# Two more chunks with all of their first layer in seven products, second weight sums in buffers of their own, some gates on GpSimd, longer filler matmuls

## The chip, the cores and the metric

The kernel runs on one core of one Trainium2 chip. A core has a matrix engine (TensorE, PE in the profile; its weight loads are PEld), three engines for elementwise work (VectorE, DVE; ScalarE, ACT; GpSimd, POOL), a queue engine (SyncE, SP) and 16 DMA engines that move data between the device memory and the core's SBUF. Matmul results land in PSUM banks, which DVE and ACT read and POOL does not.

The metric is the device time of one execution in microseconds, the median of several runs; lower is better.

## The reference

Linear attention with a cosine reweighting, and then two dense layers with a gate. All inputs are float32.

```python
# q, k, v: [8 batches, 8 heads, 576 positions, 64]
theta = pi / 2 * pos / 576
phi(x) = concat([max(x, 0) * cos(theta), max(x, 0) * sin(theta)])    # 64 -> 128
kv  = sum over s of phi(k)[s]^T v[s]                                 # 128 x 64 for each head
z   = sum over s of phi(k)[s]
att = (phi(q) @ kv) / (phi(q) @ z + 1e-6)
x   = att, heads side by side                                        # 4608 tokens x 512
h   = x @ w_in                                                       # 512 -> 2048
out = (h * cos(h)) @ w_out                                           # 2048 -> 512
```

## The kernel before

**Chunks.** Of each batch's 576 tokens 512 form a chunk of their own; the 64 that are left over of all eight batches form a ninth chunk (number 8, buffer xR). For each batch the kernel loads q, k and v (tiles qm, km, vm), makes phi with one instruction for each tile and half (`prep`, on ACT or DVE, output KQ), casts v to 16 bits (`cast_v`), forms kv and z in one product (`kv`, L371), transposes phi(q) (`q_pe` on PE for batches 0 and 1, `q_dma` as a DMA transpose later), multiplies (`num`, L433) and normalises (L449 to L453, on DVE), and transposes the result into xT (`x_pe` or `x_dma`). In batches 1, 3, 5 and 7 there is a fifth tile of q, which holds the left-over tokens of two batches.

**First layer, plain.** A column block of w_in (128 of 2048 columns) takes four matmuls of 512 columns (L562) into a PSUM bank; chunks 0 and 1 use matmuls of 256 (L530). Its gate is a Sin on ACT with a phase of a quarter turn (L503, output ch) and a multiplication (L505, `mul`) that writes gT.

**First layer in seven products.** From chunk 3 on, the dictionary FAST1 says how many of the four column groups of a chunk are formed by a Strassen-like scheme (`layer1_fast`): seven products of four 256-column matmuls (L666) take the place of four plain blocks of four 512-column ones. The scheme needs sums of parts of x (`layer1_sums`, tiles XS) and of w_in (`w_in_sums`, tiles WS): the first set (f = 0) serves groups 0 and 1, the second (f = 1) groups 2 and 3. Partial results are copied by ACT into SBUF (Y, U, Z; L674) and completed by additions on DVE (L678). Four gates follow in two narrow and one double-width multiplication: one of Y (512 columns, both inputs in SBUF, L505), one of U and Z together (1024 columns, both inputs in SBUF, L695), and one read from a PSUM bank (L505). In the kernel before, FAST1 gives two groups to chunks 3, 4, 5, 6 and 8 and four to chunk 7, and the second set of sums lies in the four buffers of the transposed q tiles (qT), since all attention is done by then.

**Second layer.** Seven products again for all chunks but the first (`layer2`, L860), with sums of the gated values (L836, L897) on DVE, or by accumulating DMAs for chunks 6 and 7 (L818). Results go to three output buffers (ost) and by DMA to the output; the stores of chunks 4, 5 and 6 add in memory (L744 and L748).

**Order of the work.** Each step of the program is recorded with `pl.add`, and two tables written out in the kernel say the rest: STARTS, a number for each step by which all steps are sorted, and ENGS, the engine of each step. So the order on each engine is fixed before the program runs, and an engine executes its list strictly in that order. Steps marked `port=True` on DVE and POOL additionally wait for each other: whenever the next marked step is on the other engine, a semaphore makes it wait for the marked step before it. DMAs are issued from the lists of SP and POOL, in order too: an issue that waits holds up what stands behind it.

**Start.** While q of batch 0 is loaded, PE runs filler matmuls on a constant tile (`warm`, L944), a second filler follows the transposes of q, and short ones stand between the first steps of `num`. The loads of w_in (four quarters, POOL queue) are held back until k of batch 0 has landed. The loads of batch 1 are held back by tiny copies on POOL (`hold_raw`, L974) that read the third quarter of w_in, the one the tables call number 2.

Of the kernel before, what the change touches and what calls it, by code (L numbers as in the profile page):

```python
# [181 lines left out]
def kernel(  # L182
# [90 lines left out]
    PAIRS0, PAIRS1 = (None, PAIRS[1]), (None, PAIRS[3])  # L273
    FILL = (4, 3, 2, 0)

    Q_PE, X_PE = (), range(1, 3)
    VCAST = ("DVE", "ACT")
    LAZY = 8.0
    LATE_BY, LATE_W = (0.0, 1.0, 3.0, 1.0), 0.6
# [111 lines left out]
    def qdst(b, t):  # L391
        return (qT[t], ("qT", t)) if t < NT else (qT4, ("qT4", 0))
# [730 lines left out]
```

## Time and profile before

| what | value |
|---|---|
| median of 3 runs | 283.02 us (282.95 to 283.87) |
| profiled execution, its own time | 285.63 us |
| span of the profiled execution, first to last instruction | 283.9 us |
| mean granted TensorE clock | 0.984 |
| PE matmuls | 2635, busy 272.2 us (96%) |
| DVE busy | 241.3 us (85%) |
| ACT busy | 205.3 us (72%) |
| POOL busy | 57.7 us (20%) |

Times of the profile are microseconds from the span's start. A line of a group names the source line, engine, operation, output and input tile, shape and count, then the busy time and the mean duration of one in ns, and then the idle time just before such instructions with what ended it. Matmuls overlap, so the mean duration of one is longer than the distance from one to the next; how many are issued in a stretch is read from the time line. A line of the time line gives start, length, engine and count; in square brackets stands the engine's idle time before it and who ended it.

### The profile page before, as it was taken

How to read it: one execution, taken by the hardware profiler on the slowest of the kernel's cores; microseconds unless marked ns; L12 is line 12 of the kernel's file. 1: busy time of each engine (PE TensorE's matmuls, PEld its weight loads, DVE VectorE, ACT ScalarE, POOL GpSimd, SP SyncE). 2: the span in 40 equal slices, each digit the busy share in tenths (PEclk: the TensorE clock that was granted, in tenths of full speed). 3: DMA queues.
4: the chain of work that ended last, by engine and by line, in shares of the span. 5: the costliest groups of instructions: out<-in, count | busy, mean ns of one | idle time of the engine just before them, and what ended most of it. 6: DMA issues, size and time to landing. Idle time of an engine off the chain costs nothing.

```text
span 283.9 us, 6672 instructions
## 1 busy us (share of the span) xinstructions
PE 272.2 (96%) x2635; PEld 210.9 (74%) x2635; DVE 241.3 (85%) x447; ACT 205.3 (72%) x357; POOL 57.7 (20%) x87
## 2 busy tenths in 40 slices
PE   7699999999999999999999999999999999999993
PEld 2557857669976677877867777787768888876882
DVE  1666798999999999997989999999998979987742
ACT  2646699589989979998988959995736687676030
POOL 1322020021500310140150102415101343230410
PEclk9599999999999999999999999999999999999998
DMA  6999989969999999999998999989323949693515
GB/s 190 316 189 241 256 270 217 354 192 242 238 341 240 262 226 191 209 339 258 291 229 199 216 324 200 220 189 163 102 57 95 180 120 110 172 134 67 113 74 148
DMA packets 80222, 58.01 MB, mean 204 GB/s; under 512 B 43200, under 2 KB 77248, under 8 KB 80192
## 3 DMA queue, kind: packets, MB, share of 16 engines
q1 hardware_dynamic: 68960, 39.99, 59.0%
q0 software_dynamic: 10496, 17.04, 28.4%
q10 hardware_dynamic: 736, 0.57, 0.7%
q8 instruction: 20, 0.33, 0.5%
q14 instruction: 10, 0.08, 0.1%
HBM read 36.75 MB, written 11.80 MB: 171 GB/s over the span
## 4 chain that ended last, share of the span: by engine, by line
PE 77%; DMA 10%; DVE 5%; ACT 3%; issue 1%; POOL 1%; SPq 1%; ACTq 0%; DVEq 0%
PE M L860 28%; PE M L562 10%; PE M L530 9%; PE M L666 9%; PE M L785 5%; PE TR L666 4%; DMA qT<-KQ 3%; DMA vm<-in_v_dram 3%; PE ATT L433 3%; PE TR L562 2%; PE ATT L371 2%; DMA qm<-in_q_dram 2%; DMA out_dram<-ost 2%; PE M L400 2%; PE ATT L944 2%
## 5 line engine op out<-in xcount | busy, mean ns | idle before, releaser
L860 PEld LDWEIGHTS <-gT 128*128 128x128 f16 x560 | 54.4, 98 | 10.1 <-issue 0.8
L503 ACT ACTIVATE ch<-M 128x512 f32<-128x512 f32 x85 | 49.8, 596 | 11.4 <-PE M L530 5.0
L860 PE MATMUL M<-w_out_sb,gT 128*128 128x256 f16 x448 | 57.1, 273 | 0.5 <-ACT ost L871 0.5
L505 DVE TENSOR_TENSOR gT<-M,ch 128x512 f16<-128x512 f32 x78 | 52.1, 685 | 5.1 <-ACT ch L503 5.0
L871 ACT ACTIVATE ost<-M 128x512 f32<-128x512 f32 x41 | 24.3, 597 | 21.8 <-PE M L860 17.7
L344 ACT ACTIVATE KQ<-km,CS 128x512 f16<-128x512 f32 x56 | 38.5, 719 | 1.3 <-DMA km<-in_k_dram 1.3
L562 PE MATMUL M<-xT,w_in_sb 128*128 128x512 f16 x160 | 39.1, 379 | 0.0
L344 ACT ACTIVATE KQ<-qm,CS 128x512 f16<-128x512 f32 x49 | 33.8, 718 | 5.2 <-DMA qm<-in_q_dram 5.2
L562 PEld LDWEIGHTS <-w_in_sb 128*128 128x128 f16 x224 | 21.1, 98 | 17.7
L860 PE MATMUL M<-T,S 128*128 128x256 f16 x256 | 32.2, 273 | 0.0
L530 PE MATMUL M<-xT,w_in_sb 128*128 128x256 f16 x256 | 30.2, 273 | 0.8 <-DVE gT L505 0.8
L360 POOL CAST V<-vm 128x1024 f16<-128x1024 f32 (+1 forms) x18 | 15.9, 912 | 68.7 <-DMA vm<-in_v_dram 24.0
L860 PEld LDWEIGHTS <-S 128*128 128x128 f16 x256 | 24.8, 98 | 4.1
L530 PEld LDWEIGHTS <-w_in_sb 128*128 128x128 f16 x256 | 24.4, 98 | 4.4 <-issue 0.7
L666 PEld LDWEIGHTS <-w_in_sb 128*128 128x128 f16 x216 | 20.7, 98 | 3.4
L453 DVE TENSOR_TENSOR x<-ATT,rec 128x512 f16<-128x512 f32 x32 | 22.1, 692 | 1.3 <-DVE rec L451 0.2
L731 POOL DMA_DIRECT2D out_dram<-ost x20 | 10.8, 545 | 48.8 <-ACT ost L871 35.9
L678 DVE TENSOR_TENSOR Z<-M,Z 128x512 f32<-128x512 f32 x26 | 17.6, 686 | 2.4 <-PE M L666 1.2
L433 PEld LDWEIGHTS <-qT 128*128 128x128 f16 (+1 forms) x320 | 14.3, 101 | 5.1 <-issue 1.9
L674 ACT ACTIVATE Z<-M 128x512 f32<-128x512 f32 x22 | 12.9, 597 | 6.6 <-PE M L666 6.4
L748 POOL DMA_DIRECT2D out_dram<-ost x12 | 6.7, 566 | 52.9 <-ACT ost L871 52.9
L503 ACT ACTIVATE ch<-TR 128x512 f32<-128x512 f32 x17 | 10.2, 599 | 9.4 <-PE TR L666 5.0
(144 smaller groups left out, 473.8 us busy)
## 6 DMA issues: line engine op xcount, KB each, us to landing
out_dram<-ost POOLq DMA_DIRECT2D x38, 256.0 KB, 4.0
qm<-in_q_dram SPq DMA_DIRECT2D x8, 640.0 KB, 6.7
km<-in_k_dram SPq DMA_DIRECT2D x8, 640.0 KB, 7.0
qm<-in_q_dram SPq DMA_DIRECT2D x8, 512.0 KB, 5.7
km<-in_k_dram SPq DMA_DIRECT2D x8, 512.0 KB, 5.3
vm<-in_v_dram SPq DMA_DIRECT2D x6, 640.0 KB, 7.4
vm<-in_v_dram SPq DMA_DIRECT2D x6, 512.0 KB, 7.0
w_in_sb<-in_moe_w_in_dram POOLq DMA_DIRECT2D x4, 512.0 KB, 9.1
```

Source lines behind the costliest of these rows:

```text
L344: fn = {"ACT": lambda: nc.scalar.activation(out=out_, in_=in_, func=AF.Relu, scale=sc), "DVE": lambda: nc.vector.tensor_scalar(out=out_, i ...
L360: "POOL": lambda: nc.gpsimd.tensor_copy(out=out_, in_=in_)}
L433: nc.tensor.matmul(bank[hb][ps, hh * D1:(hh + 1) * D1], lhsT=x[:, h, :], rhs=z[:, h, :], start=True, stop=True)
L453: nc.vector.tensor_tensor(out=split(x16[n][:, hs, :], k), in0=A[:, :, :, 0:D], in1=split(rec[n][:, hs], k).unsqueeze(3).broadcast_to((P, k ...
L503: act(0.5, due, lambda: nc.scalar.activation(out=ch[c], in_=bank, func=AF.Sin, bias=math.pi / 2.0, scale=1.0), [key], [("ch", c)])
L505: mul(due, 0.61, lambda q: q.tensor_tensor(out=dst, in0=bank if len(dst.shape) == 2 else bank.rearrange("p (j s) -> p j s", j=dst.shape[1] ...
L530: nc.tensor.matmul(M1[m][:, jj * 2 * P:(jj + 1) * 2 * P], lhsT=w_in_sb[:, cc, j * P:(j + 1) * P], rhs=X[:, cc, ts], start=(cc == 0), stop= ...
L562: nc.tensor.matmul(M, lhsT=w_in_sb[:, cc, j * P:(j + 1) * P], rhs=X[:, cc, :], start=(cc == 0), stop=(cc == NCT - 1))
L666: nc.tensor.matmul(bank[0][:, j * TH:(j + 1) * TH], lhsT=a(cc, j), rhs=b[:, cc, :], start=(first and j == 0 and cc == 0), stop=(last and j ...
L678: dve(0.61, due + 0.3, lambda: nc.vector.tensor_tensor(out=dst, in0=bank[0], in1=dst, op=ALU.add), [bank[1], key], [key])
L860: nc.tensor.matmul(bank[0][:, tt * MH:(tt + 1) * MH], lhsT=a[:, j, tt * P:(tt + 1) * P], rhs=b[:, j, :], start=(first and (apart or tt == ...
L871: act(0.5, due, lambda: nc.scalar.activation(out=dst, in_=view(bank), func=AF.Copy), [bank[1]], dk)
```

## The change

- **FAST1**: chunk 6 and chunk 8 form all four groups in seven products, as chunk 7 did. 16 plain blocks become four groups of seven products.
- **w_in's second sums** get buffers of their own (WSB2 to WSB4, and a part of w_in that is no longer read), and are formed ahead of chunk 6 where they were formed ahead of chunk 7. To make room, the fifth tile of transposed q has no buffer of its own any more (qT4 is gone): it uses that of tile 0. Its transpose is therefore recorded after the products of the other tiles.
- **Gates on GpSimd**: the multiplications of Y and of U with Z may be on DVE or POOL, and the tables say which. 10 of 18 gates of Y and 5 of 18 of U with Z are on POOL: in chunk 8 four of Y and two of U with Z, the others in chunks 3 to 7.
- **Filler**: the first from 14 to 28 matmuls, the second from 16 to 17.
- **The tables** are new as a whole, 1363 steps where there were 1335, so the order changes on every engine. PE has 2698 matmuls for 2635. At the start the order is now: filler, transposes of q tiles 3 and 0, second filler, transpose of tile 1, first half of `kv`, second half, transpose of tile 2, `num`; before, all four transposes stood ahead of the second filler and `kv` behind it. DVE's and ACT's copies of transposed q stand behind k's preparations and v's casts, where two of them stood between. w_in's quarters are loaded in the order 0, 1, 3, 2 (before: 2, 0, 1, 3), with the first half of w_out behind them and `hold_raw`, which waits for quarter 2, behind that. After batch 1's `kv` PE now has one transpose, four halves of `num`, one transpose and then a step of the second layer; before, two transposes, the same halves of `num` and that step.

The diff, with the two tables left out:

```diff
@@ -241,7 +244,6 @@
     KQ = sb("KQ", [P, 2, (NT + 1) * H * 2 * D])
     kp, qp = [KQ[:, n].rearrange("p (t h g d) -> p t h g d", t=NT + 1, h=H, g=2) for n in range(2)]
     qT = [sb(f"qT{t}", [P, H, P]) for t in range(NT)]
-    qT4 = sb("qT4", [P, H, P])
     kvz = [sb(f"kvz{n}", [P, H, D1]) for n in range(2)]
     NX = 4
     den = [sb(f"den{n}", [P, H], F32) for n in range(NX)]
@@ -273,7 +275,7 @@
     PAIRS0, PAIRS1 = (None, PAIRS[1]), (None, PAIRS[3])
     FILL = (4, 3, 2, 0)
 
-    Q_PE, X_PE = (), range(1, 3)
+    X_PE = range(1, 3)
     VCAST = ("DVE", "ACT")
     LAZY = 8.0
     LATE_BY, LATE_W = (0.0, 1.0, 3.0, 1.0), 0.6
@@ -389,7 +391,7 @@
                 out=Z, in_=ATT[:, :, 0:HB * D1], func=AF.Copy), keys, zk)
 
     def qdst(b, t):
-        return (qT[t], ("qT", t)) if t < NT else (qT4, ("qT4", 0))
+        return qT[t % NT], ("qT", t % NT)
 
     def q_pe(b, t, bank, key, eng, due):
         dst, dkey = qdst(b, t)
@@ -488,14 +490,11 @@
     m1n, chn, m2n = [0], [0], [0]
 
     def mul(due, cost, fn, rd, wr, pool):
-
         if pool is None:
             dve(cost, due, lambda: fn(nc.vector), rd, wr)
-        elif pool:
-            pl.add("POOL", 0.15 + 1.9 * cost, 0.3 + 1.9 * cost, due, lambda: fn(nc.gpsimd), rd, wr,
-                   port=True)
         else:
-            dve(cost, due, lambda: fn(nc.vector), rd, wr, port=True)
+            either(due, {"DVE": cost, **({"POOL": 0.15 + 1.9 * cost} if pool else {})},
+                   {"DVE": lambda: fn(nc.vector), "POOL": lambda: fn(nc.gpsimd)}, rd, wr)
 
     def gate(bank, key, dst, dkeys, due, pool=None, rd=()):
         c = chn[0] % NCH
@@ -566,23 +565,25 @@
              rd=["KQ"] if c == B else [])
 
 
-    FAST1 = {3:2,4:2,5:2,6:2,7:4,8:2}
+    FAST1 = {3:2,4:2,5:2,6:4,7:4,8:4}
     SUMS_AT = min(FAST1) - 1
-    Y_POOL, UZ_POOL = (), ()
+    Y_POOL, UZ_POOL = range(B + 1), range(B + 1)
     CH2, JF = NCT // 2, JH * P // 2
 
 
     WSA = {1: w_in_sb[:, 0:CH2, 2 * JF:3 * JF]}
     for n in (2, 3, 4):
         WSA[n] = sb(f"WS{n}", [P, CH2, JF])
-    LATE = any(nf > 2 for nf in FAST1.values())
+    LATE = min(c for c, nf in FAST1.items() if nf > 2)
+    assert all(FAST1[c] == NJT // 4 for c in range(LATE, NC))
 
     def flat(t, dt=F16):
         v = t.rearrange("p a b c -> p (a b c)") if len(t.shape) == 4 else t.rearrange(
             "p a b c d -> p (a b c d)")
         return v if dt == F32 else v.bitcast(F16)
-    WSB = {n: qT[n - 1].rearrange("p h s -> p (h s)").rearrange("p (c f) -> p c f", c=CH2)
-           for n in range(1, 5)}
+    WSB = {1: w_in_sb[:, 0:CH2, 3 * JF:4 * JF]}
+    for n in (2, 3, 4):
+        WSB[n] = sb(f"WSB{n}", [P, CH2, JF])
 
     Z3 = [sb("Z3", [P, 3 * SM], F32)]
     XSS = [[sb(f"XS{i}", [P, CH2, TH]) for i in range(4)]]
@@ -600,9 +601,9 @@
 
         def tt(n, a, b, op, rd, wr):
             dve(0.61, due, lambda: nc.vector.tensor_tensor(out=ws[n], in0=a, in1=b, op=op),
-                [("w_in", f), ("w_in", 2 + f)] + rd, wr + [("WS", n, f)] + ([("qT", n - 1)] if f else []), lazy=20.0, port=True)
+                [("w_in", f), ("w_in", 2 + f)] + rd, wr + [("WS", n, f)], lazy=20.0, port=True)
         tt(3, a11, a21, ALU.subtract, [], [])
-        tt(1, a21, a22, ALU.add, [], [] if f else [("w_in", 2)])
+        tt(1, a21, a22, ALU.add, [], [("w_in", 2 + f)])
         tt(2, ws[1], a11, ALU.subtract, [("WS", 1, f)], [])
         tt(4, a12, ws[2], ALU.subtract, [("WS", 2, f)], [])
 
@@ -988,7 +989,7 @@
         for i, nm in enumerate("kv"):
             dve(0.53, i - 9, lambda nm=nm: nc.vector.memset(raw[nm][:, :, NT, :], 0.0), [],
                 hk(nm, ts=[NT]))
-        warm(14, 6.5)
+        warm(28, 9.05)
         for nm in ORDER0:
             load(0, nm, 0, HALVES if nm == ORDER0[2] else (slice(0, H),))
         weights()
@@ -996,7 +997,7 @@
             prep(0, "q", t, 0, "DVE", t)
             prep(0, "q", t, 1, "DVE" if t == 1 else "ACT", t)
             q_pe(0, t, *BANKS[t], "ACT" if t % 2 else "DVE", t)
-        warm(16, 3.45, rd=[("TR", 0)])
+        warm(17, 3.67, rd=[("TR", 0)])
         for t in range(NT + 1):
             prep(0, "k", t, 0, "DVE", 4)
             prep(0, "k", t, 1, "DVE" if t == 2 else "ACT", 4)
@@ -1027,13 +1028,16 @@
             due = T + 2 + t + 6 * (t > 1)
             for g in range(2):
                 prep(1, "q", t, g, "DVE" if g == 0 else "ACT", due)
-            q_pe(1, t, *BANKS[t % 2], "ACT" if t % 2 else "DVE", due)
+            if t < NT:
+                q_pe(1, t, *BANKS[t % 2], "ACT" if t % 2 else "DVE", due)
         for hb in range(2):
             for t in range(NT + 1):
                 cast_v(1, t, "ACT" if t % 2 else "DVE", T + 4 + hb, HALVES[hb])
         kv(1, T + 6)
         for t in range(NT + 1):
             due = T + 8 + t if t < NT else start[1] + 12
+            if t == NT:
+                q_pe(1, t, *BANKS[t % 2], "ACT" if t % 2 else "DVE", due - 2)
             n = num(1, t, due, PAIRS1[t % len(PAIRS1)])
             x_pe(1, t, n, *BANKS[t % 2], "ACT", due)
 
@@ -1051,12 +1055,12 @@
             due = T + 8 + 1.2 * t
             for g in range(2):
                 prep(b, "q", t, g, "", due)
-            if b in Q_PE:
-                q_pe(b, t, TR, ("TR", 0), "ACT" if t % 2 else "DVE", due + 1)
-            else:
+            if t < NT:
                 q_dma(b, t, due + 1)
         for t in list(range(NT)) + ([NT] if b % 2 else []):
             due = start[b] - 9 + 1.2 * t if t < NT else start[b]
+            if t == NT:
+                q_dma(b, t, due - 3)
             n = num(b, t, due)
             if b in X_PE:
                 x_pe(b, t, n, TR, ("TR", 0), "ACT", due)
@@ -1074,7 +1078,7 @@
             attention(c)
         if c == SUMS_AT + 1:
             w_in_sums(0, start[c] - 12)
-        if c == B - 1 and LATE:
+        if c == LATE:
             w_in_sums(1, start[c] - 6)
         layer2(c - 1)
         layer1(c)
```

More of the change, by code (lines that the diff above doesn't have):

```diff
@@ L117 @@
     "DDPSSSSSSSSGGGGGGGGDAPDDDPADAPDDAPAPDADADDDADADADADDADADPPADPPDPPAPPDPPAPPDPPAPPDPAPADPADP"
-    "ADPADPADPADPADPADPADPADPADPADPADPADPADPADGSSGSSGGGGGSSSSDADADADADADAPDDAPADAPDDAPADAPDDADA"
-    "DDADADPPAPPDPAPPDPAPPDPAPPDPAPPDPAPAPAPAPAPDPDGGPDPDGGPADPADPADPADPADPADPADPADPADPADPADPAD"
-    "PADPADPADPADDDDDSSSSSSAADDADADDAGGGPPADDSAASADSDASPPDPAPPDPAPPDPAPPDPADDDPPAPPDDPPAPPAPPDP"
-    "PDGGPPAGGPADPADPADPADPADPADPADPADPADPADPADPADPADPADPADPADSSSSSSAAAAAAADADGGGPPAAASADSAASAD"
-    "SAASPPDSPPDSPPDSPPDSPPDSDDDDDDDPPAPPDDPPAPPAPPDPPDGGPPAGGDDDDPAPDADPAPAPDPDADPADPADPADPADP"
@@ L129 @@
-    "DDDDDDSPPAPPAGGPPAGGPPAPPAPPAGGPPAGGGGDDDDPAPDADPAPAPDPDADPADPAPDADPAPAPDPDADPADPAPDADPAPA"
-    "PDPDADPADPAPDADPAPAPDPDADPADDDDDSPPAPPDGGPPAPPAPPDPPDGGPPAGGDDDDPAPDADPAPAPDPDADPADPADPADP"
-    "ADPADPAPDADPAPAPDPDADPADPADPADPADPADDDDDDDPPAPPDDDPPAPPAPPDPPDSASAAPPDSADSA"
+    "ADPADPADPADPADPADPADPADPADPADPADPADPADPADGSSGSSGGGGGSSSSDADADADADADAPDDAPADAPDDAPADADADADD"
+    "ADADPPAPPDPAPPDPAPPDPAPPDPAPDPPDPAPAPAPAPAPDPDGGPDPDGGPADPADPADPADPADPADPADPADPADPADPADPAD"
+    "PADPADPADPADDDDDSSSSSSADADAADDAAGGGPPADASDDSAASAASPPDPAPPDPAPPDPAPPDPADDDPPAPPDDPPAPPAPPDP"
@@ new lines @@
+    "PDGGPPAGGPADPADPADPADPADPADPADPADPADPADPADPADPADPADPADPADSSSSSSDDAAAAAAAAGGGPPADASAASDASAA"
+    "SADPPDSPPDSPPDSPPDSSPPDSDDDDDDDPPAPPDDPPAPPAPPDPPDGGPPAGGDDDDPAPDAGPAPAPDPDADPADPADPADPADP"
+    "ADPAPDAGPAPAPDPDADPADPADPADPADPADSSSSSSAAAAAADAAAGGGPPAAASAASAASADSPPDSPPDSPPDSPPDSDDDPPAP"
+    "PDDPPAPPAPPDPPDGGPPAGGDDDDPAPDAGPAPAPDPDADPADPADPADPADPADPAPDADPAPAPDPDADPADPADPADPADPADSS"
+    "SSSSDDAAAAAAADGGGPPAADSAASDDSAASAAPPDSPPDSPPDSPPDSSPPDSDDDPPAPPADPPAGGPPAPPAPPAGGPPAGGGGDD"
+    "DDPAPDAGPAPAPDPDADPADPADPADPADPADPAPDADPAPAPDPDAGPADPADPADPADPADSSSSSSAAAAAAADAAGGGPPAAASA"
@@ new lines @@
+    "DSADSAASPPDSPPDSPPDSPPDSDDDDDDDPPAPPADPPAGGPPAPPAPPAGGPPAGGGGDDDDPAPDADPAPAPDPDADPADPAPDAG"
+    "PAPAPDPDAGPADPAPDADPAPAPDPDADPADPAPDADPAPAPDPDADPADSSSSSSDAAAAAAAAAGGGPPADASDASAASDDSAAPPD"
+    "SPPDSPPDSPPDSSPPDSDDSPPAPPAGGPPAGGPPAPPAPPAGGPPAGGGGDDDDPAPDAGPAPAPDPDAGPADPAPDADPAPAPDPDA"
+    "DPADPAPDADPAPAPDPDADPADPAPDADPAPAPDPDADPADDDDDSPPAPPDGGPPAPPAPPDPPDGGPPAGGDDDDPAPDAGPAPAPD"
+    "PDAGPADPAPDAGPAPAPDPDAGPADPAPDAGPAPAPDPDADPADPAPDAGPAPAPDPDADPADDDDDDDPPAPPDDDPPAPPAPPDPPD"
+    "SASAAPPDSADSA"
```

6 lines of the change are left out of this document (removed), and 194 rows, old and new, of the table STARTS.

## Prediction

> **What bounds the kernel now.** I read the page first: TensorE (PE) is busy for 96% of the span, and its idle times are few.
>
> ```profile
> span 283.9 us, 6672 instructions
> PE 272.2 (96%) x2635; PEld 210.9 (74%) x2635; DVE 241.3 (85%) x447; ACT 205.3 (72%) x357; POOL 57.7 (20%) x87
> PEclk9599999999999999999999999999999999999998
> ```
>
> Then the table of windows, for the start and three long stretches (busy us, then instructions; the last three columns are granted clock, DMA share, GB/s):
>
> ```profile
> 5.10:8.50 3.40, 1.26 (x6) 0.39 (x4) 0.14 (x1) 0.17 (x1) 0.00 (x0) 1.00 1.02 359
> 8.50:15.30 6.80, 5.92 (x38) 4.28 (x39) 5.60 (x13) 5.46 (x10) 3.27 (x5) 0.50 0.93 272
> 46.00:130.00 84.00, 83.58 (x896) 62.57 (x893) 79.58 (x154) 72.84 (x128) 14.57 (x20) 1.00 1.05 258
> 130.00:188.00 58.00, 57.48 (x563) 45.42 (x563) 53.73 (x98) 50.70 (x90) 10.59 (x16) 1.00 1.03 237
> 188.00:278.00 90.00, 90.00 (x825) 74.52 (x824) 76.63 (x123) 52.28 (x91) 24.21 (x30) 1.00 0.60 118
> ```
>
> From 46 us on PE misses under 1 us in all, so there a microsecond taken from PE's list is a microsecond gained, as long as DVE (85 to 95% busy) and POOL keep up. Before 46 us it is another matter: PE waits for data, and from 8.5 to 15.3 us it has half its clock. The time line of PE shows what that costs:
>
> ```profile
> 9.38 1.01 PE L400 MATMUL TR<-IDENT,KQ 128*128 128x128 f16 x8 [3.02 <-DVE KQ L345]
> 10.19 2.76 PE L400 MATMUL M<-IDENT,KQ 128*128 128x128 f16 x24
> 12.75 4.90 PE L944 MATMUL ATT<-S 128*128 128x512 f16 x16
> 17.48 1.38 PE L371 MATMUL M<-V,KQ 128*128 128x65 f16 x40
> 23.67 1.04 PE L530 MATMUL M<-xT,w_in_sb 128*128 128x256 f16 x8
> ```
>
> The 16 filler matmuls (L944) hold PE until 17.3 us, though v has landed (13.2 us its first heads, 14.7 us the rest, by the landing records). Last, the groups by shape, for the gates and for POOL:
>
> ```profile
> L505 DVE TENSOR_TENSOR gT<-M,ch 128x512 f16<-128x512 f32 x78 | 52.1, 685 | 5.1 <-ACT ch L503 5.0
> L695 DVE TENSOR_TENSOR gT<-Z,ch 128x1024 f16<-128x1024 f32 x9 | 11.0, 1220 | 0.2 <-ACT ch L689 0.2
> L360 POOL CAST V<-vm 128x1024 f16<-128x1024 f32 x12 | 12.5, 1057 | 55.5 <-DMA km<-in_k_dram 20.8 <-DVE den L449 18.5 <-DMA vm<-in_v_dram 10.8
> L360 POOL CAST V<-vm 128x512 f16<-128x512 f32 x6 | 3.7, 620 | 13.2 <-DMA vm<-in_v_dram 13.2
> L744 POOL DMA_DIRECT2D out_dram<-ost x12 | 12.2, 1383 | 6.7 <-ACT ost L871 4.1 <-DMA out_dram<-ost 2.6
> ```
>
> The sum is made against the profiled execution: span 283.9, its own time 285.63, so 1.7 lie around the span. It is 2.6 above the median of the three runs, 283.02; I subtract the same difference from the median. About 0.3% (0.85 us) is what a measurement of this kernel can tell from no change.
>
> **Part 1, seven products.** Two column groups each of batch 6 and of the last chunk change. Plain: 16 matmuls of 512 columns, issued 8 in 1.73 us, 3.45. Seven products: 28 of 256 columns, 8 in 0.874, 3.06. Four groups: **-1.6 us** of PE. Their weight loads (98 ns) fit under a 109 ns matmul. ACT gets +1.7 a group (three copies and a wide Sin against four Sins), beside PE: 17 of 27 us busy at 188 to 215, 14 at 242 to 269. DVE gets 4.65 for 2.74 a group (three additions at 0.69, gates 0.68, 1.22 and 0.69), +7.6; ten gates of 512 and five of 1024 leave it for POOL, -12.9. So DVE gets 5 us shorter, though not in each stretch: at 188 to 215 it is busy 26.3 of 27. The second sums (4 at 0.6) only move earlier.
>
> **Part 2, the start.** The first filler goes from 14 to 28 matmuls. In this trace nine ran at 0.427 until 5.1 us, later ones take 0.216: 28 end at 5.1 + 19 x 0.216 = 9.2 us, just ahead of the transposes that wait for q's preparation until 9.38. In the trace the clock fell after a stretch (5.1 to 8.5) in which PE was busy for 1.26 us of 3.40; now that stretch is full, and I expect the clock to stay at 1.0. Then, by the new order: two transposed tiles at 0.46 (to 10.3), 17 fillers at 0.216 (to 14.0), a third tile (14.4). DVE no longer copies a q tile between k's preparations: five at 0.40 from 11.6, three casts at 0.2, one preparation, 14.7; ACT ends its share at 14.8. kv starts at 14.9 instead of 17.48, and its second half at 15.5. From kv to the first layer the trace has 6.2 us (17.48 to 23.67); the new order moves one more tile transpose into waits there, so the first layer starts at about 21.4 for 23.67.
>
> What is late next? Batch 1's loads. They wait, behind a POOL instruction, for quarter 2 of w_in, which is now the fourth load, not the first. The first two quarters landed at 18.1 and 20.7, 2.6 apart while nothing else ran; so the fourth lands at 25.9, where loads were issued from 18.8 before. The first half of w_out needs 5.2 more at that rate, k, q and v 10.5 (batch 0's three took 11.9 with 2 of latency): last v at 41.6, against 42.3 before. The order is worse, the end no later. PE by its own list reaches batch 1's second kv half at 21.4 + 0.46 + 16 x 0.87 + 3 x 1.73 + 2 x 0.46 + 0.62 = 42.5, plus 1.1 of idle as before: 43.6. Before it was 46.18, with 0.46 more work ahead: 2.1 gained. Then a loss: before, a second-layer step of 1.73 stood early enough to cover kvz's copy and the normalisations; now part of it is bare, 0.2 to 1.5, I take 0.8. Net **-1.3 us**; from both sides 0 (v late by 2 us, or the clock halved after all) and -2.4.
>
> **Part 3, gates on POOL.** The trace has no two-input operation on POOL. From below: DVE's own rows, 0.68 and 1.22. From above: two casts that read as much, 2 x 0.62 = 1.24 and 2 x 1.06 = 2.11. I take the upper ends, since a cast of equal reads on the same engine is the nearest row. Each gate stands in one line with DVE's instructions marked for the shared port: the next marked one on DVE waits for POOL, and all DVE behind it. Nine of the fifteen lie in chunks 3 to 7, one or two to a chunk: such a turn is some 0.6 (1.24 less 0.68) to 0.9 us longer than DVE's own, which the 5 us that DVE is spared hide. The tight place is the last chunk: by the program's order PE has, between its first POOL gate and the first second-layer product that needs the last one, 18 first-layer products at 0.44 and eight second-layer steps at 0.87, 14.9 us, of which about 14.5 lie after that gate's start; POOL's queue holds 4 gates of 512, 2 of 1024, a pair of accumulating DMAs (2.47 by the pair at 249.4) and two single ones (1.38): 4.96 + 4.22 + 2.47 + 2.76 = 14.4. It just fits: **+0.2**, from 0 to +1.5. The Trainium skill, GPSIMD Engine Reference, section 3.1, measures a two-input addition at 1.96 times DVE's time: 1.34 and 2.39 here as an estimate, 15.4 us for that queue, and the sum would be 0.8 higher.
>
> **Part 4, batch 1, 3, 5 and 7's fifth q tile** now reuses the first tile's buffer: it waits for that tile's products, and SP's queue (loads and transposes behind it) with it. In the trace this transpose took SP 1.3 us at 96.3 and 3.3 at 145.3. The tile's result feeds only the last chunk, but the next batch's first transpose waits for its matmuls. From 0 to +1.0 (the trace's PE idle at 121 to 153, 1.3 in all, came from such late transfers); a gain is possible too, -0.5, since loads are now spread between transposes. I take 0.
>
> **Sum**: -1.6 - 1.3 + 0.2 + 0 = -2.7: 282.9 for the profiled execution, span 281.2, and **280.4** beside the median.
>
> **Rivals.**
> *Front given back.* The clock still halves at 8.5 us, or batch 1's loads end 2 us late. With the clock halved the 17 fillers end at 16.8 and kv starts at 17.4, as before; only -1.6 + 0.2 stay: **281.6**. For it: loads start 7 us later and DMA share there is over 1.0. Against: last v by bytes.
> *First filler cold for longer.* If the clock rises 3.4 us later, 8 more matmuls cost 0.21 each: the filler ends at 10.9, the transposes 1.5 later, kv near 16.0: **281.4**. The trace had it up at 5.1. The Trainium skill, TensorE: Matmul & The Clock Gate, Part 1, says why it could: the window of 3413 ns runs free, so its place differs from run to run. The half clock here lasted 6.8 us, two windows, and agrees.
> *POOL decides (slower).* If a gate of 512 costs 1.75 or more (2.5 times DVE's), 1024 3.5, the last chunk's queue is 19.2 us for 14.5 of PE: +4.7, less 0.5 of slack; with -2.9 from the rest 283.0 + 4.2 - 2.9 = **284.3**. It ends above 283.9 from about 1.7 a gate. Against: the cast rows. The Trainium skill, GPSIMD Engine Reference, section 4.1, speaks against the change: elementwise work of two inputs belongs on VectorE, GpSimd being about twice as slow; that is short of 2.5 times.
> *Late transposes.* Part 4 at its worst is +1.0; and at 188 to 215 DVE, 26.3 of 27 us busy, gets batch 6's two groups, +3.8, less 1.9 for the one pair of gates that POOL takes there: +1.9 where its 0.7 of idle hides none, +1.5 taken. Together +2.5: **282.9**, no change.
>
> **How the numbers follow.** Forecast 0.50, front given back 0.16, cold filler 0.08, POOL 0.16, late transposes 0.10. The first three are faster by over 0.3%; a fifth of the last is too, and its rest lies within 0.3%; the POOL case is slower: faster 0.76, same 0.08, slower 0.16. The range starts at 279.2 (front at its bound, -2.4, with -1.6 and no cost for POOL or transposes is 279.0) and ends at 283.4, leaving out most of the POOL case; the forecast's own range is 279.4 to 281.4.
>
> **What would show it.** Granted clock 1.0 from 5.1 us on; the first filler ending near 9.2; batch 0's kv matmuls at 15 and the first layer at 21 to 22; batch 1's last v cast by 43.5; 2698 matmuls; a POOL TENSOR_TENSOR row near 1.2 and 2.1; PE idle after 60 us still near 1 us. A half clock after 8.5, PE waiting on POOL in the last chunk, or on qT transposes, would make it wrong.

## The result, and the profile after

The kernel after takes 282.01 us (median of 22 runs, 281.50 to 284.31), the kernel before on the same chip 283.33 (22 runs, 282.16 to 286.08). The ratio is 0.9949, with a 95% interval from 0.9932 to 0.9967: faster by 0.5%, some 1.4 us. The forecast was 280.4, so 2.6 below the median then known; the direction is right, the time lies inside the range, and the gain is about half of what was forecast.

The profiled execution of after has a span of 279.7 us and its own time is 281.59. Beside the profiled execution of before (283.9 and 285.63) the span is 4.2 less, more than the 2.7 of the sum. Between profiled executions the gain is larger than the sum, between medians it is smaller, and that contradiction is what the runs below take apart.

The page of after, its first lines and the clock:

```profile
span 279.7 us, 6825 instructions
PE 272.6 (97%) x2698; PEld 215.5 (77%) x2698; DVE 236.9 (85%) x442; ACT 210.2 (75%) x363; POOL 82.9 (30%) x102
PEclk9999999999999999999999999999999999999999
```

The 2698 matmuls are there, DVE is 4.4 us shorter (241.3 to 236.9), and the granted clock has no dip left. The table of windows of after (length, busy us and instructions of PE, PEld, DVE, ACT and POOL, then granted clock, DMA share, GB/s):

```profile
5.10:8.50 3.40, 3.40 (x13) 1.37 (x12) 1.25 (x4) 1.27 (x3) 0.00 (x0) 1.00 1.08 362
8.50:15.30 6.80, 6.80 (x53) 3.85 (x52) 5.59 (x16) 4.58 (x10) 3.65 (x5) 1.00 1.06 278
46.00:130.00 84.00, 84.00 (x878) 62.94 (x876) 79.69 (x153) 73.11 (x129) 17.27 (x22) 1.00 1.08 272
130.00:188.00 58.00, 58.00 (x584) 45.91 (x582) 54.28 (x99) 50.86 (x89) 16.60 (x21) 1.00 0.94 215
188.00:278.00 90.00, 86.98 (x826) 77.09 (x824) 70.66 (x114) 55.57 (x94) 40.42 (x38) 1.00 0.67 127
```

From 5.1 to 8.5 us PE is full, where it was busy for 1.26 us of 3.40, and the stretch after it runs at a clock of 1.00 for 0.50. (PE's 86.98 in the last window is no idle time: this execution ends its work before 278.) The time line of PE at the start:

```profile
1.32 9.04 PE L945 MATMUL ATT<-S 128*128 128x512 f16 x28 [1.32 <-POOL S L931]
10.20 0.61 PE L402 MATMUL TR<-IDENT,KQ 128*128 128x128 f16 x8
11.09 3.83 PE L945 MATMUL ATT<-S 128*128 128x512 f16 x17
15.21 1.37 PE L373 MATMUL M<-V,KQ 128*128 128x65 f16 x40
21.20 1.03 PE L529 MATMUL M<-xT,w_in_sb 128*128 128x256 f16 x8
```

The first filler ends at 10.2 us, not at 9.2; kv of batch 0 starts at 15.2 (17.5 before) and the first layer at 21.2 (23.7 before), as forecast. The groups by shape, for the gates on GpSimd:

```profile
L504 POOL TENSOR_TENSOR gT<-Z,ch 128x512 f16<-128x512 f32 x5 | 6.3, 1268 | 56.6 <-ACT ch L502 20.0 <-DVE gT L837 15.6 <-PE ATT L435 15.1
L696 POOL TENSOR_TENSOR gT<-Z,ch 128x1024 f16<-128x1024 f32 x2 | 4.7, 2352 | 8.8 <-DVE gT L504 8.7
```

A gate of 512 columns takes 1.27 us on GpSimd and one of 1024 takes 2.35, where I had taken 1.24 and 2.11. By DVE's own rows in this trace (685 and 1220 ns) that is 1.85 and 1.93 times DVE. The Trainium skill, GPSIMD Engine Reference, section 3.1, has 1.96 for a two-input addition. For the gate of 1024 its 2.39 came nearer than the cast row that I used (2.11); for the gate of 512 the cast row did (1.24, where 1.96 times DVE is 1.34).

### The profile page after: what moved, and what is told of

It is laid out like the page before. It is cut to its first block, busy times and chain, and to the rows that moved or that the text cites. A ratio compares the mean times of both kernels' runs of the same rounds, so it can differ in the third digit from the quotient of the medians.

```text
span 279.7 us, 6825 instructions
## 1 busy us (share of the span) xinstructions
PE 272.6 (97%) x2698; PEld 215.5 (77%) x2698; DVE 236.9 (85%) x442; ACT 210.2 (75%) x363; POOL 82.9 (30%) x102
## 4 chain that ended last, share of the span: by engine, by line
PE 92%; ACT 3%; DVE 2%; issue 1%; POOL 0%; ACTq 0%; POOLq 0%
PE M L861 34%; PE M L667 14%; PE M L561 11%; PE M L529 9%; PE TR L667 6%; PE ATT L945 5%; PE ATT L435 3%; PE M L786 3%; PE ATT L373 3%; PE TR L561 2%; ACT KQ L346 2%; DVE x L455 1%; PE M L402 1%; PE M L373 0%; PE TR L475 0%
## 5 line engine op out<-in xcount | busy, mean ns | idle before, releaser
L504 DVE TENSOR_TENSOR gT<-M,ch 128x512 f16<-128x512 f32 x73 | 48.5, 685 | 5.9 <-ACT ch L502 5.7
L502 ACT ACTIVATE ch<-M 128x512 f32<-128x512 f32 x75 | 43.4, 596 | 12.0 <-PE M L529 5.4
L346 ACT ACTIVATE KQ<-qm,CS 128x512 f16<-128x512 f32 x46 | 31.5, 720 | 4.1 <-DMA qm<-in_q_dram 4.1
L561 PE MATMUL M<-xT,w_in_sb 128*128 128x512 f16 x136 | 33.8, 379 | 0.0
L362 POOL CAST V<-vm 128x1024 f16<-128x1024 f32 (+1 forms) x18 | 15.9, 907 | 50.8 <-DVE den L451 20.7
L679 DVE TENSOR_TENSOR Z<-M,Z 128x512 f32<-128x512 f32 x31 | 21.1, 687 | 4.3 <-PE M L667 3.1
L561 PEld LDWEIGHTS <-w_in_sb 128*128 128x128 f16 x160 | 14.9, 98 | 12.2
L504 POOL TENSOR_TENSOR gT<-Z,ch 128x512 f16<-128x512 f32 x5 | 6.3, 1268 | 56.6 <-ACT ch L502 20.0
L690 ACT ACTIVATE ch<-Z 128x1024 f32<-128x1024 f32 x12 | 12.7, 1057 | 6.9 <-DVE Z L679 4.8
L675 ACT ACTIVATE Z<-M 128x512 f32<-128x512 f32 x26 | 15.1, 596 | 3.4 <-PE M L667 2.4
L435 PE MATMUL ATT<-kvz,qT 128*128 128x65 f16 (+1 forms) x288 | 16.0, 195 | 0.8 <-DVE x L455 0.5
```

Of the source, the lines that this page charges most:

```text
L346: fn = {"ACT": lambda: nc.scalar.activation(out=out_, in_=in_, func=AF.Relu, scale=sc), "DVE": lambda: nc.vector.tensor_scalar(out=out_, i ...
L362: "POOL": lambda: nc.gpsimd.tensor_copy(out=out_, in_=in_)}
L435: nc.tensor.matmul(bank[hb][ps, hh * D1:(hh + 1) * D1], lhsT=x[:, h, :], rhs=z[:, h, :], start=True, stop=True)
L502: act(0.5, due, lambda: nc.scalar.activation(out=ch[c], in_=bank, func=AF.Sin, bias=math.pi / 2.0, scale=1.0), [key], [("ch", c)])
L504: mul(due, 0.61, lambda q: q.tensor_tensor(out=dst, in0=bank if len(dst.shape) == 2 else bank.rearrange("p (j s) -> p j s", j=dst.shape[1] ...
L561: nc.tensor.matmul(M, lhsT=w_in_sb[:, cc, j * P:(j + 1) * P], rhs=X[:, cc, :], start=(cc == 0), stop=(cc == NCT - 1))
```

## The theories

**Theory A**: the profiled execution of before was a bad one. Its q landed at 8.2 us and PE lost half its clock for 6.8 us, and most executions do not pay for that. So the start's gain was sized on what is lost only sometimes, and in the median little more than the seven products is left. **Theory B**: the start's gain is there in every execution, and something later eats it, GpSimd's gates or DVE. The text recorded ahead of the first four runs puts numbers on both.

| kernel | median us | ratio to before, 95% interval |
|---|---|---|
| after | 282.01 | 0.9949 (0.9932 to 0.9967) |
| before again | 283.86 | 0.9994 (0.9959 to 1.0029) |
| before, long fillers | 282.97 | 0.9969 (0.9938 to 0.9999) |
| after, short fillers | 282.73 | 0.9967 (0.9933 to 1.0000) |
| after, gates on DVE | 285.51 | 1.0074 (1.0032 to 1.0117) |
| after, last chunk's gates on DVE | 282.97 | 0.9989 (0.9966 to 1.0012) |
| after, four groups plain | 284.56 | 1.0047 (1.0020 to 1.0073) |
| after, w_in early | 281.32 | 0.9926 (0.9901 to 0.9950) |
| after, w_in early, filler 22 | 280.87 | 0.9909 (0.9876 to 0.9942) |
| after, filler 22 alone | 282.36 | 0.9948 (0.9928 to 0.9969) |
| after, w_in earliest, filler 22 | 280.73 | 0.9893 (0.9870 to 0.9916) |
| before, long fillers, w_in early | 282.47 | 0.9960 (0.9936 to 0.9984) |
| after again | 282.00 | 0.9936 (0.9913 to 0.9959) |
| after, halves together | 281.47 | 0.9911 (0.9881 to 0.9941) |
| w_in earliest, filler 22, again | 280.72 | 0.9890 (0.9856 to 0.9923) |
| the same, halves together | 280.29 | 0.9884 (0.9844 to 0.9924) |

The kernel before was measured anew beside each set of runs; its medians lie between 282.94 and 284.07. Differences of half a microsecond between two variants lie inside these intervals; where I read one below, a trace carries it.

## The experiments

### Is the clock lost in every execution?

The kernel before as it is:

> The kernel before, unchanged, to see what its executions share with the profiled one (span 283.9, clock 0.984, own time 285.63 against a median of 283.3). Theory A, that the profiled execution was a bad one: the cold matmuls and the half clock at the start are in some executions only; the median stays at 283.3 +-0.4, spans spread from about 280.5 to 284, and the span follows the granted clock (0.995 and above: under 282; 0.985 and below: over 283). Theory B, that the lost clock is in every execution: all show a clock near 0.984 and the spans lie within 1 us of each other.

Measured: 283.86 us, ratio 0.9994. The profiled execution had a span of 282.1 and a clock of 0.989. Its windows, in the same columns:

```profile
5.10:8.50 3.40, 1.94 (x6) 0.58 (x4) 0.54 (x2) 0.57 (x1) 0.00 (x0) 1.00 1.03 363
8.50:11.90 3.40, 2.91 (x33) 2.75 (x34) 2.21 (x6) 2.07 (x5) 0.27 (x2) 0.70 1.08 358
11.90:15.30 3.40, 3.40 (x14) 1.38 (x13) 3.40 (x8) 3.40 (x8) 3.08 (x4) 0.80 0.85 199
```

Here the clock is low for about half as long (0.70 and 0.80 over 3.4 us each, where the first profile had 0.50 over 6.8), q landed at 7.8 for 8.2, kv of batch 0 starts at 15.90 for 17.48 and the first layer at 22.08 for 23.67. So two executions of one kernel differ by 1.6 us ahead of the first layer, more than the 1.3 us that I had put down for the whole of Part 2. The median, 283.86, is just above what theory A expected (283.3 +-0.4). Of 46 executions of before, this run's and those beside these first four kernels, 11 with a mean clock under 0.9945 have a median span of 282.2, 21 with 0.9975 and above have 281.0. The second half of theory A's expectation did not hold: spans at a full clock still go from 280.4 to 284.3, so the clock goes with about 1.2 us of the spread and not with all of it.

Now the fillers of after in the kernel before (the diff), and the other way round, those of before in after:

```diff
-        warm(14, 6.5)
+        warm(28, 9.05)
-        warm(16, 3.45, rd=[("TR", 0)])
+        warm(17, 3.67, rd=[("TR", 0)])
```

> The kernel before with the two fillers of the kernel after (28 and 17 matmuls) and nothing else. It holds the clock through 5.1 to 8.5 us. Theory A: the median falls little, 282.6 to 283.3 (0 to -0.7), its spread gets narrower and the clocks are 0.995 and above. Theory B, that the front is worth 1.3 us in every execution and the gain is lost later: 281.3 to 282.0, at least 1.3 below before.

> The kernel after with the fillers of before (14 and 16 matmuls). Theory A: the median stays within 0.5 us of after's (281.6 to 282.5), with more executions of a lower clock (0.985 to 0.99) and longer spans among them. Theory B: 1.3 us or more above after, 283.3.

Measured: 282.97 for the first (0.9 below before again and 0.65 below the 283.62 of the other runs of before beside it, spans of 280.4 to 282.1, no clock under 0.995) and 282.73 for the second (0.7 above after, three of twelve clocks between 0.989 and 0.994). By the medians the fillers are worth some 0.7 us in both, where Part 2 has 1.3 for the start; that is theory A's side, with a little more than it gave the short fillers (0.5). But the interval of the first all but reaches 1, that of the second overlaps after's, and the two traces do not show the gain. With long fillers in before, the first layer starts 0.6 earlier than in before again, PE then waits 0.55 us for w_out at 49.4, and chunk 3's first product comes at 104.22 for 104.09. With short fillers in after, the first layer starts at 20.37, earlier than after's 21.20, and batch 1's q lands at 38.61 for 37.86. So 0.7 is what two medians suggest, and no more.

### GpSimd's gates back on DVE

Theory B's other suspect. The 15 gates stay where they are in the order, but on DVE:

```diff
+ON_POOL = (516, 547, 661, 817, 858, 989, 999, 1141, 1151, 1253, 1263, 1272, 1282, 1291, 1310)
+ENGS = "".join("D" if n in ON_POOL else e for n, e in enumerate(ENGS))
```

> The kernel after with its 15 GpSimd gates given back to DVE, in the same places of the same order. Theory A, in which the GpSimd gates cost PE nothing and the 12.9 us they spare DVE hide: 281.6 to 282.5, as after, with DVE busy 250 for 237. Theory B, in which the front's gain is eaten by GpSimd's turns later: 281.0 or less, 1 us below after. A third case, that DVE could not carry the seven products of batch 6 and the last chunk alone: 282.8 or more.

Measured: 285.51 us, 3.5 above after. Theory B falls: taking GpSimd's turns away costs time and gains none. The case that I had only added as a third is the one that came, and by more than it said. Without GpSimd the change is slower than before. The trace shows where, in the list of PE's waits from 100 us on:

```profile
PE ATT L438 <- DVE x L458: 1.1, 1, 1.1
PE M L670 <- DVE vm L682: 0.4, 1, 0.4
PE ATT L438 <- DMA qT<-KQ: 0.3, 1, 0.3
PE M L670 <- DVE XS L627: 0.2, 1, 0.2
```

and on PE's time line:

```profile
206.35 0.32 PE L438 MATMUL ATT<-kvz,qT 128*64 128x65 f16 x8 [1.13 <-DVE x L458]
252.47 0.60 PE L670 MATMUL M<-xR,w_in_sb 128*128 128x256 f16 x4 [0.41 <-DVE vm L682]
```

The same list of after is empty. The first wait is for the last normalisation of batch 7, the second for an addition in the last chunk, the fourth for a sum of x; the third is for a late transfer and has nothing to do with the gates. By the distances from each matmul's start to the next, PE pauses 2.8 us longer from 90 us on than in after, some 2.3 of it around the waits for DVE and 0.5 at the transfer. DVE's time line ahead of the first wait:

```profile
203.44 0.68 DVE L682 TENSOR_TENSOR Z<-M,Z 128x512 f32<-128x512 f32 x1
204.04 1.22 DVE L699 TENSOR_TENSOR gT<-Z,ch 128x1024 f16<-128x1024 f32 x1
205.17 0.16 DVE L454 TENSOR_SCALAR den<-ATT 128x8 f32<-128x8 f32 x1
205.60 0.69 DVE L458 TENSOR_TENSOR x<-ATT,rec 128x512 f16<-128x512 f32 x1
```

The double-width gate of chunk 6 at 204.04 is one of those that GpSimd has in after; the normalisation stands right behind it, and PE's wait of 1.1 us is about that gate's length. The stretch from 188 to 215 us, first of after, then of this run:

```profile
188.00:215.00 27.00, 27.00 (x282) 23.88 (x281) 25.38 (x47) 17.90 (x32) 11.51 (x12) 1.00 0.76 133
```

```profile
188.00:215.00 27.00, 25.87 (x272) 22.96 (x269) 25.96 (x46) 17.55 (x31) 5.99 (x8) 1.00 0.68 123
```

DVE is busy 25.96 us of 27 and PE waits; with 0.6 us less on DVE, after does not. So DVE is the bound here as soon as it has to take GpSimd's part. Only the last chunk's six gates on DVE (the diff is against the run before):

```diff
-ON_POOL = (516, 547, 661, 817, 858, 989, 999, 1141, 1151, 1253, 1263, 1272, 1282, 1291, 1310)
+ON_POOL = (1253, 1263, 1272, 1282, 1291, 1310)
```

> The kernel after with the six GpSimd gates of the last chunk on DVE, the nine of chunks 3 to 7 left on GpSimd. All 15 on DVE cost 3.5 us (285.5 for 282.0). If the cost goes with the place where DVE was late in that run's trace (stages of chunk 3, of chunk 6 and of chunk 8, 0.8, 1.2 and 0.85): 282.7 to 283.3. If the last chunk alone carries it: 284.5 or more. If it carries none: 281.7 to 282.3.

Measured: 282.97, 1.0 above after: the first case. In its trace PE pauses 0.85 us longer than in after from 90 us on, all of it between 247 and 252 us, where it waits 0.4 for an addition again (vm, L682). By subtraction the other nine gates carry the other 2.5. Against what I had feared (*POOL decides*), the last chunk's queue on GpSimd holds. Its time line in after:

```profile
244.59 1.62 POOL L504 TENSOR_TENSOR KQ<-qm,ch 128x512 f16<-128x512 f32 x1
245.81 1.96 POOL L819 DMA_DIRECT2D gT<-S  x1
246.77 1.94 POOL L819 DMA_DIRECT2D S<-S  x1
247.35 3.75 POOL L696 TENSOR_TENSOR KQ<-qm,ch 128x1024 f16<-128x1024 f32 x1
249.68 2.65 POOL L504 TENSOR_TENSOR KQ<-vm,ch 128x512 f16<-128x512 f32 x1
250.91 2.40 POOL L745 DMA_DIRECT2D out_dram<-ost  x1
253.08 1.55 POOL L504 TENSOR_TENSOR KQ<-Z,ch 128x512 f16<-128x512 f32 x1
254.31 1.28 POOL L745 DMA_DIRECT2D out_dram<-ost  x1
255.00 2.99 POOL L696 TENSOR_TENSOR KQ<-vm,ch 128x1024 f16<-128x1024 f32 x1
257.32 1.89 POOL L504 TENSOR_TENSOR KQ<-km,ch 128x512 f16<-128x512 f32 x1
```

The spans on POOL overlap; what counts is the distance to the next start, 1.22 to 1.23 for a gate of 512 and 2.32 to 2.33 for one of 1024. From the first gate's start at 244.59 to the last one's at 257.32, and 1.23 more, the queue holds 14.0 us (14.6 to the end that the line gives the last gate), for 14.4 in the sum. PE's first second-layer product that reads the last chunk's gates (KQ) starts without a wait, and the ones behind it do too:

```profile
259.10 1.91 PE L861 MATMUL M<-w_out_sb,KQ 128*128 128x256 f16 x16
```

### The seven products

> The kernel after with groups 2 and 3 of chunks 6 and 8 plain again (16 blocks of four 512-column matmuls for 4 groups of seven products); their two GpSimd gates go with them, 13 are left. All else stays, the second weight sums too, so that half of the 16 plain blocks read weights which those sums have overwritten: the output of chunks 6 and 8 is not the reference's, the work is. Theory A, that the products' 1.5 us of TensorE are gained whole and what was over-estimated is the start: 283.3 to 283.8 beside 282.0 for after. Theory B, that copies, additions and gates take back most of the products' gain: 282.6 or less.

```diff
-    FAST1 = {3:2,4:2,5:2,6:4,7:4,8:4}
+    FAST1 = {3:2,4:2,5:2,6:2,7:4,8:2}
...
```

(Not shown are the lines that make groups 2 and 3 of chunks 6 and 8 plain and keep the second sums ahead of chunk 6, and the two tables, written anew with 1335 steps for 1363: the order is another one on every engine.)

Measured: 284.56, 2.5 above after. That is on theory A's side, and more than it said. In its trace the last matmul comes 3.05 us later than in after. By the distance from each matmul's start to the next, the 16 plain blocks take PE 13.90 us and the four groups of seven products that replace them in after 12.33: 1.57 is PE's own work. Waits for gates in and around chunk 7's two layers and chunk 5's second one add 0.94; they belong to the order that I wrote for the plain blocks, not to the products. Three waits that have to do with loads and transfers add 0.92 (0.33 near 39 us for batch 1's q, 0.26 near 49 for w_out, 0.33 at 146), and the first filler is 0.38 shorter. So the run gives the products their 1.5 and no exact value above it.

### What sets the pace up to 50 us

The times of one execution of each kernel, from the time line of PE and the landing records (us): when kv of batch 0 starts, when the first layer starts, when the last of batch 1's q lands, when kv of batch 1 starts, and the distance of the last two.

| kernel | kv, batch 0 | first layer | q, batch 1, landed | kv, batch 1 | distance |
|---|---|---|---|---|---|
| before | 17.48 | 23.67 | 39.23 | 45.58 | 6.35 |
| before again | 15.90 | 22.08 | 38.85 | 43.99 | 5.14 |
| before, long fillers | 15.29 | 21.47 | 37.99 | 43.38 | 5.39 |
| after | 15.21 | 21.20 | 37.86 | 42.25 | 4.39 |
| after again | 14.38 | 20.71 | 38.10 | 42.46 | 4.36 |
| after, short fillers | 13.77 | 20.37 | 38.61 | 42.97 | 4.36 |

In three executions of the order of after kv of batch 1 starts 4.36 to 4.39 us behind the landing of q, whether the first layer began at 20.4 or at 21.2. So it does in the traces of the two runs with gates on DVE and of the one with four plain groups (4.35 to 4.36). PE that is earlier at the start only waits longer at 39 us. That gave a new theory: in after the loads set the pace of the start. Two kernels pull the loads forward, the second one also PE. The loads of w_in are held back by a tiny copy on GpSimd that reads k of batch 0; now it reads a tile that a q preparation has written:

```diff
-                in_=raw[ORDER0[1]][0:2, 0, 0, 0:1].broadcast_to((2, 4)))
-        pl.add("POOL", 0.4, 0.5, 0, hold, hk(ORDER0[1], [0], [0]), [("w_in", g) for g in range(4)])
+                in_=qp[0:2, 1, 0, 0, 0:1].broadcast_to((2, 4)))
+        pl.add("POOL", 0.4, 0.5, 0, hold, [("qp", 1, 0, 0)], [("w_in", g) for g in range(4)])
...
-        warm(28, 9.05)
+        warm(22, 7.75)
```

(The last pair of lines in the second kernel alone; the call that records the copy and the loads stands behind q's preparations, and the five steps of w_in's loads get earlier numbers in STARTS.)

> The kernel after with the loads of w_in held back until a q preparation of batch 0 is done (9.3 us) and not until k has landed (10.5): every load behind them is issued 1.2 us earlier. Theory A, that the start up to 50 us is set by the loads' bytes, so that a PE that starts earlier waits for them: 281.1 to 281.7, last v of batch 1 near 39.8 for 40.9. Theory B, that PE's own list sets the start: 281.8 to 282.3, no change.

> The last kernel with a first filler of 22 matmuls for 28, which ends near the time at which the first q preparations are done (8.1 to 8.5). Theory A (PE and the loads both move up): 280.6 to 281.3, batch 0's kv near 14.3, first layer near 20.5. Theory B (the order of loads or the clock takes it back, as in the run with fillers of 14 and 16): 282.0 or more.

Measured: 281.32 and 280.87, 0.7 and 1.1 below after. Both went as theory A of these runs says. In the trace of the first, q lands at 36.56, 1.3 earlier than in after, but that execution's first filler is as long as in after (10.3 us) and kv of batch 1 starts at 42.23 as there, 5.67 behind q: now PE's list sets it. Its span, 279.7, is that of after's profiled execution, so no trace shows where the 0.7 of the median is gained. With the filler of 22, q lands at 36.87, kv of batch 0 starts at 13.75, and kv of batch 1 at 41.23, 4.36 behind q again; chunk 3's first product comes at 102.96, 1.0 earlier than in after.

The filler alone, with the loads where after has them:

> The kernel after with a first filler of 22 matmuls for 28 and the loads where they were: TensorE gets to the transposes of q some 1.3 us earlier, the loads come as before. If the loads set the pace up to 50 us: 281.7 to 282.5, no gain, and TensorE waits for batch 1's q near 39 us. If TensorE's own list does: 281.2 or less, the part of the last kernel's gain that the filler brought (its earlier loads alone gave 281.3, with this filler 280.9).

Measured: 282.36, ratio 0.9948, no gain. The first layer starts at 20.37, as early as in the short-filler run; kv of batch 1 at 42.08, 4.36 behind q's landing at 37.72. The time line shows PE waiting for the preparation of batch 1's q, here and in the second run of after:

```profile
39.46 0.61 PE L402 MATMUL M<-IDENT,KQ 128*128 128x128 f16 x8 [0.50 <-DVE KQ L347]
```

```profile
39.84 0.61 PE L402 MATMUL M<-IDENT,KQ 128*128 128x128 f16 x8 [0.53 <-DVE KQ L347]
```

So the two must move together: a filler that ends earlier gains nothing (282.36), loads that come earlier gain 0.7, both together 1.1. One step more, w_in released by the very first q preparation:

> Filler of 22, and the loads of w_in released by the first q preparation (7.9 us), 1.5 us earlier again than in the kernel that gave 280.9. Loads set the pace: 280.0 to 280.6. Now k and v of batch 0 share the queue engines with w_in and land later, so that kv of batch 0 starts after 14.5 instead of 13.75: 281 or more.

Measured: 280.73 (280.66 to 280.84), just above what I expected, and no better than the run before it by more than 0.1: w_in is issued at 8.6 for 9.8, but its first quarter lands at 16.2 for 15.9, probably because k and v are still coming in. Batch 0's kv is hardly later (13.87). No more was gained this way.

The kernel before with long fillers and early loads:

> The kernel before with the fillers of after (28 and 17) and the loads of w_in released by a q preparation (9.5 us for 10.7), nothing else of after. With the fillers alone it gave 282.97 beside 283.6. If before's start too is set by loads: 0.6 less than that, ratio to before 0.994 to 0.996. If by TensorE's list: ratio 0.9965 to 0.998, as with the fillers alone.

Measured: 282.47, ratio 0.9960. It is at the edge of the load-bound case, and its interval (0.9936 to 0.9984) holds both. In the trace kv of batch 1 is 6.21 behind q: in before's order PE's list sets this point, with 1 to 2 us to spare against the 4.36 of after's order. It does not settle what the early loads are worth there.

The kernel after once more, as a control:

> The kernel after, unchanged, beside the others on the same chip: ratio to before 0.995 as in its first runs, clocks 0.996 and above, and the spans within 279.5 to 281.

Measured: 282.00, ratio 0.9936; the spans lie from 279.4 to 280.8, and one clock is at 0.995.

### Where the rest of the products' gain goes

By the order lists PE has 1.6 us less to do in after. Yet from the first product of chunk 3 to the end PE pauses for 1.2 us in after (both traces) where the quietest traces of before pause for 0.4 to 0.5. (A pause is what the distance from one matmul's start to the next has beyond its usual length.) About half of the difference stands at the fifth q tile's products in batches 3, 5 and 7. The time line of before, then of after, around batch 3's:

```profile
103.56 0.45 PE L433 MATMUL ATT<-kvz,qT 128*64 128x65 f16 x16
```

```profile
98.67 0.32 PE L435 MATMUL ATT<-kvz,qT 128*64 128x65 f16 x8
98.93 1.04 PE L561 MATMUL M<-xT,w_in_sb 128*128 128x512 f16 x4
99.89 0.32 PE L435 MATMUL ATT<-kvz,qT 128*64 128x65 f16 x8
```

In before the two halves stand behind one another; the tables of after put one to four other steps between them. Each time PE passes into such a half and out of it, it loses about 0.1 us (the four 512-column matmuls at 98.93 should be issued in 0.86 us and the next one starts at 99.89, 0.96 later), so a parted pair costs 0.2 more. Put together again, in after and in the best kernel so far, by three numbers in STARTS (10084 to 9973, 15363 to 15164, 20689 to 20446):

> The kernel after with the same three pairs put together, nothing else. By the pauses: 281.3 to 281.7 beside 282.0, ratio to before 0.002 below after's. If they are covered: 282.0 as after.

> The kernel with w_in released first and a filler of 22 (280.73), with one thing more: in batches 3, 5 and 7 the two halves of the fifth q tile's products stand behind one another on TensorE, as they did in before, where after puts 1 to 4 other steps between them. If each parted pair costs the extra 0.2 us that the traces show (0.38 of pauses for 0.19): 280.0 to 280.3, 0.5 less. If those pauses are covered anyway: 280.6 to 280.9.

> The kernel with w_in released by the first q preparation and a filler of 22 once more, to stand beside the two others on the same chip: 280.6 to 280.9, ratio to before 0.989 to 0.991.

Measured: 281.47 for after with the halves together (0.5 below after), 280.29 for the best kernel with them and 280.72 without, on the same chip. Both are what the pauses say, 0.4 to 0.5. The intervals are wider than that, and of the six runs of the best kernel with them one took 282.74, so that by the means it gains 0.1; it is the traces that show the cause. The time line of after with the halves together (line numbers are 22 lower there, because the tables are broken into lines differently):

```profile
98.77 0.45 PE L413 MATMUL ATT<-kvz,qT 128*64 128x65 f16 x16
99.16 1.90 PE L539 MATMUL M<-xT,w_in_sb 128*128 128x512 f16 x8
```

The sum of PE's pauses from 90 us on falls from 1.53 us in after to 0.96.

The version with w_in released by the first q preparation, a first filler of 22 and the halves together beats both kernels: 280.29 us, ratio to before 0.9884 (0.9844 to 0.9924). By these intervals it cannot be told from the same version without the halves (0.9890).

## Why the prediction was half right

- **Part 1, the products (-1.6): right.** Between the traces of before with long fillers and of after, PE spends 13.81 us on the plain blocks of chunks 6 and 8 (from each start to the next) and 12.33 on what replaces them, -1.48. Taking them out again costs at least that. Chunk 7's first layer got 0.3 slower (12.23 to 12.55), in three short waits, two for DVE and one for ACT (0.07, 0.17 and 0.10 between 224 and 232 us), that I had not priced.
- **Part 2, the start (-1.3): the step that failed, not in its mechanism but in what it was measured against.** Against the profiled execution it was if anything too small: clock 1.0 from 5.1 us, kv at 15.2 (forecast 14.9), first layer at 21.2 (21.4), first layer of chunk 1 at 50.27 for 52.84. But that execution of before is not typical: q 0.4 us later and the low clock twice as long as in the next one. I noted that it was 2.6 above the median and then "subtract the same difference from the median", which takes for granted that a typical execution has as much to gain. It has not. Against the execution of before again, chunk 3's first product comes at 103.98 and 104.24 in two traces of after for 104.09, with 0.37 us more of PE's work ahead of it: 0.2 to 0.5 us gained, and the medians of the runs on fillers say 0.7. So the term was -1.3 and the runs show -0.2 to -0.7. What is late next, the loads of batch 1, I named and worked out (last v at 41.6; it landed at 40.9), but the one that PE waits for is q, whose last part lands at 37.9 to 38.1 and is needed 1.7 us ahead of the transposes at 39.6 to 39.8.
- **Part 3, GpSimd (+0.2): the queue was right, the gate of 1024 a little low.** 14.0 to 14.6 us for 14.4, 2.33 for 2.11, and no wait. What the sum did not show is how much hangs on it: the same gates on DVE cost 3.5 us. I wrote that DVE gets 5 us shorter; the right reading is that the products could not be had without it.
- **Part 4, the fifth q tile (0): the change costs 0.4 to 0.5 there, and not where I looked.** The reused buffer brings no wait in the trace of after. The products of this tile were parted by the new order, which the order lists show and I did not price.
- **Outside the span**: own time less span is 1.8 us in before and 1.9 to 2.1 in after and its variants (medians of each set of runs); 0.2 that I had put at nothing. Its cause was not looked for.

The recorded sum was 0.1 off in itself: 283.02 less 2.7 is 280.3, not 280.4.

Together: -1.5 for the products, -0.2 to -0.7 for the start, +0.3 for chunk 7, +0.5 for the parted halves, +0.2 outside the span: -0.7 to -1.2, for 1.3 to 1.4 measured. The rest fits waits for late transfers behind 50 us which some traces of before show and others not (0.66 at 129 and 0.61 at 147 us in the first, 0.88 at 121 in the second, none in two more with long fillers); with so few traces that is argued and not shown.

Of the rivals, *front given back* was nearest (281.6 for 282.0), and in part by luck: loads and not PE end up setting the start, but neither of its conditions came. The clock was held, and last v landed at 40.9, earlier than the 41.6 of the sum. *First filler cold for longer* happened in the profiled execution (10.2 us for 9.2) and cost nothing there, because q's landing sets the same point. *POOL decides* did not come, nor did *late transposes*.

## What to carry to other kernels

Before an estimate is carried to the median, look whether the profiled execution is one: a lost clock or a late load in it is a gain that most executions do not have. When PE is made earlier at a start that is full of loads, ask what it will wait for next, and move the loads with it; a filler alone gained nothing here, with the loads 1.1 us. And a step that is to take work off PE may only be possible if another engine is relieved in the same change: undo the relief in thought, and see which engine becomes the bound.

## What the hardware showed that I had not expected

- The matmuls of the first filler start 0.427 us apart at first and 0.216 from some point on, and that point differs from execution to execution. In the nine traces with 28 of them 8 to 14 are slow, and the filler takes 7.9 to 9.0 us. In all 17 traces the change comes between 4.3 and 7.2 us from the span's start, 2.9 us apart. The granted clock of the windows does not show it: it is 1.00 from 5.1 to 8.5 us in after, where the slow spacing lasts until 7.2. The Trainium skill, TensorE: Matmul & The Clock Gate, Part 1, gives the transition a free-running window of 3413 ns and a variation of 500 ns to either side; the 2.9 us fit into one such window, but not into 500 ns to either side. The low clock of before also came in one such length or two (some 3.4 us by its 0.70 and 0.80 over two stretches of 3.4, and 6.8).
- A set of the fifth q tile's 65-column matmuls, whose weights are 128*64, costs PE about 0.1 us going in (the matmul ahead of it takes 310 ns to the next start for 216, or 203 for 109) and 0.1 coming out, so 0.2 for each separate set. It is not the 65 columns: sets with weights of 128*128 stand between the same 512-column and 256-column matmuls in the same traces, and there the distances stay 216 and 109 ns going in and 30 to 33 inside and coming out.
- A two-input product of float32 on GpSimd, written as 16 bits, takes twice DVE's time even in a full queue: 1.22 to 1.23 us (512 columns) and 2.31 to 2.33 (1024) from start to start, where DVE's own stand 0.60 and 1.13 apart. The spans that the profile gives on GpSimd go up to 3.75, and DVE's are 0.685 and 1.22, so spans of the two engines are not to be compared.
